# Half of one input loaded by sixteen transfers of eight partitions instead of one of 128

## The chip, the cores and the metric

One core of a Trainium2 chip. The metric is the device time of one execution in microseconds (us). A run counts as fast when it lies within 1.5% of the fastest of its kernel. Ratios are the mean time of one kernel's fast runs over the mean of the other's fast runs of the same rounds, so they are not quite the ratio of the medians quoted beside them.

## The reference, cut to what matters

```python
def _attn_ref(q, k, v):                      # each (8, 8, 576, 64) float32
    phi = lambda x: np.where(x > 0, x, np.exp(x) - 1.0) + 1.0
    q_p, k_p = phi(q), phi(k)
    kv = np.einsum('bhsd,bhse->bhde', k_p, v);  z = np.sum(k_p, axis=2)
    num = np.einsum('bhsd,bhde->bhse', q_p, kv)
    den = np.einsum('bhsd,bhd->bhs', q_p, z)[..., None] + 1e-06
    return num / den
# then: rfft over the sequence, 64 modes times complex 512 x 512 weights
# (moe_w_r, moe_w_i: 134 MB in float32), irfft, residual, u + relu(u @ w_ch)
```

The kernel reads 164 MB from memory, 134 MB of it the two weight arrays.

## The kernel before

GpSimd issues nearly all loads; they convert float32 to a 16-bit type on the way. Batch 0's q is the exception: SyncE loads it as float32 in two halves (c = 0 and 1), and then the identity and the DFT table.

```python
    def load(b):
        for nm, src in (("q", q), ("k", k), ("v", v)):
            ...
            if (nm, b) == ("q", 0):
                for c in range(2):
                    t = sA.tile([128, 2, NJ * Dh], F32, tag="x16", bufs=2, name=f"q32_{c}")
                    pin(nc.sync.dma_start(out=t, in_=rows_in[:, :, c * NJ * Dh : (c + 1) * NJ * Dh]))
                    raw[nm, b, c] = t
                pin(nc.sync.dma_start(out=id16, in_=id16_dr.ap()))
                pin(nc.sync.dma_start(out=fwd_sb, in_=fwd_dr.ap()))
                continue
            t = sA.tile(shape, F16, tag=f"{nm}16", bufs=2, name=f"{nm}16_{b}")   # two buffers
            pin(nc.gpsimd.dma_start(out=t, in_=rows_in))
    ...
    def exps(b):                 # ScalarE: exp of q, then of k
        for nm in ("q", "k"): ...
    def features(b):             # VectorE: max, min of q, then of k, then the copy of v
        for nm in ("q", "k"): ...

    load(0); load(1)
    exps(0); features(0); exps(1)
    for b in range(B):
        load(b + 2)              # its k waits until batch b's k buffer is free
        ...                      # [cut]
```

`pin` keeps the order of the program on each engine. The k load of batch 2 ("k2" below) reuses the buffer of batch 0's k. So it waits until VectorE has finished batch 0's `ke`, and VectorE does q first. Everything that GpSimd loads afterwards waits behind k2.

Of the kernel before, what the change touches and what calls it, by code (L numbers as in the profile page):

```python
# [16 lines left out]
NJ = 9  # L17
# [26 lines left out]
def kernel(  # L44
# [10 lines left out]
    nc = tc.nc  # L55

    B, H, S, Dh = q.shape
# [50 lines left out]
    pin = tc.keep_in_program_order  # L108
# [69 lines left out]
    def load(b):  # L178
        for nm, src in (("q", q), ("k", k), ("v", v)):
            rows_in = src[b].rearrange("h s d -> (h s) d").rearrange(  # L180
                "(hp r j) d -> r hp (j d)", r=128, j=2 * NJ if nm == "q" else NJ
            )
            if (nm, b) == ("q", 0):
                for c in range(2):
                    t = sA.tile([128, 2, NJ * Dh], F32, tag="x16", bufs=2, name=f"q32_{c}")
                    pin(nc.sync.dma_start(out=t, in_=rows_in[:, :, c * NJ * Dh : (c + 1) * NJ * Dh]))
                    raw[nm, b, c] = t
                pin(nc.sync.dma_start(out=id16, in_=id16_dr.ap()))
                pin(nc.sync.dma_start(out=fwd_sb, in_=fwd_dr.ap()))
                continue  # L190
            shape = [128, 2, 2 * NJ * Dh] if nm == "q" else [128, NHP, NJ * Dh]
            t = sA.tile(shape, F16, tag=f"{nm}16", bufs=2, name=f"{nm}16_{b}")
            pin(nc.gpsimd.dma_start(out=t, in_=rows_in))
            raw[nm, b] = t
# [157 lines left out]
    def transform(b, dc):  # L352
# [17 lines left out]
        if dc == NDC - 1:  # L370
# [3 lines left out]
            pin(nc.scalar.mul(out=xv[:, :, 0, :], in_=xf[:, :, 1, :], mul=-1.0))  # L374

    load(0)
    load(1)
    exps(0)
    for _ in features(0):
        pass  # L380
    exps(1)
    for b in range(B):
        if b + 2 < B:
            load(b + 2)
            if b % 2 == 1:
                w_next()
        turn_q(b, 0)
        turn_q(b, 1)
        sum_kv(b)
        if b + 1 < B:  # L390
            for _ in features(b + 1):
                pass
        if b + 2 < B:
            exps(b + 2)
        for jj in range(NJJ + 1):
            form_x(b, jj)
            if b == 0 and jj == 0:
                make_place()
            if b > 1 and jj == 1:
                place_x(b - 2)  # L400
            if b > 0 and jj in (2, 3):
                transform(b - 1, jj - 2)
        if b > 0:
            transform(b - 1, 2)
            transform(b - 1, 3)
# [153 lines left out]
    def x_of(t: int):  # L559
        if t < B * NJJ:  # L560
            return x_main[t // NJJ][:, t % NJJ, :]
        i = t - B * NJJ
        return x_tail[i // 2][:, i % 2, :]
# [364 lines left out]
    for h, eng in enumerate((nc.sync, nc.gpsimd)):  # L928
        eng.dma_start(
            out=YZ_all[64 * h : 64 * h + 64 : NF // NL].rearrange("r b z d -> r b (z d)"),  # L930
            in_=last.rearrange("p z d -> p (z d)"),
# [10 lines left out]
    def add_one(n: int, i: int):  # L942
# [8 lines left out]
            out=x_of(0), in0=accs[0][:, 0], scalar=0.0, in1=x_of(0), op0=ALU.max, op1=ALU.add  # L951
# [51 lines left out]
```

## Time and profile before

| | us |
|---|---|
| median (runs) | 425.01 (423.59 to 425.35) |
| second exp of batch 0's q starts | 6.19 |
| GpSimd issues k2 | 14.61 |
| last engine ends GpSimd's sixth load | 23.38 |

From the page of the kernel before: the busy share of the 16 DMA engines in 40 slices (9 is 90% or more), the GB/s written in each slice, SyncE's queue with its packets, and the chain of waits by engine.

```profile
DMA  9999999999999999999999999999999999995697
GB/s 215 209 209 215 207 221 201 224 209 221 218 217 221 208 215 220 218 211 217 218 217 212 221 215 217 214 219 217 215 215 216 218 212 218 218 209 113 235 400 309
q1 hardware_dynamic: 4256, 11.22, 7.2%
DMA 69%; PE 16%; DVE 4%; ACT 4%; issue 3%; POOL 2%; DVEq 0%; POOLq 0%; ACTq 0%
```

The DMA engines are the bound. Mostly they write 16-bit data and read float32, so where some 210 GB/s are written, twice as much is read. Only about the last four of 40 slices look different.

From the timeline of the kernel before, the instructions that the change touches (start, duration, engine and line, output and input, and what the engine had waited for):

```profile
0.74 0.95 SPq L186 DMA_DIRECT2D q<-in_q_dram  x2
...
6.19 1.16 ACT L213 ACTIVATE qe<-q 128x1152 f16<-128x1152 f32 x1 [0.36 <-DMA q<-in_q_dram]
...
14.61 0.77 POOL L193 DMA_DIRECT2D k<-in_k_dram  x1 [8.80 <-DVE ke L226]
...
20.28 0.98 POOL L193 DMA_DIRECT2D q<-in_q_dram  x1 [4.14 <-DVE qe L226]
```

One more reading is needed. A load is split over the DMA engines, each of which writes a completion packet of four bytes when its share is done. The trace's packet records show these, but they don't name the engine. As long as the engines are less than one load apart (2.8 us), sorting by time gives each load's first and last engine. Where they come further apart, the completions of two loads mix. There the sixth load is told by its interval: it is a q load of 16 rows of 2304 bytes per engine and comes 2.79 us after the fifth on the same engine, while a k or v load of 32 rows of 1152 bytes takes 2.84 us.

### The profile page before, as it was taken

Reading aid. Unit: us, or ns where it says so; the run is one execution under the profiler, and the core shown is the slowest. Engines: PE = TensorE matmul, PEld = TensorE weight load, DVE = VectorE, ACT = ScalarE, POOL = GpSimd, SP = SyncE. Lnnn points to the kernel's source line nnn. Section 1 sums busy time; section 2 is a strip of 40 time slices with the busy share of each in tenths; the row PEclk is TensorE's granted clock in tenths of the full one; section 3 lists DMA queues with packets and bytes.
Section 4 is the critical chain, followed back from the end, with each engine's and each line's share of the span. In section 5 each row is a group of like instructions: output and inputs, shape, how many; then the busy total and the mean of one; then the engine's idle time right before and its main releaser. Section 6 shows DMA issues by size and latency. Waiting matters only on the chain.

```text
span 423.3 us, 7890 instructions
## 1 busy us (share of the span) xinstructions
PE 268.8 (63%) x3378; PEld 146.1 (35%) x3378; DVE 215.2 (51%) x447; ACT 161.4 (38%) x253; POOL 57.0 (13%) x99
## 2 busy tenths in 40 slices
PE   1358376778417645444344778869687785997992
PEld 0247355566202322222122323324243332463320
DVE  4599489994203453354444444445353424431793
ACT  4687588844202102000000244435253432330781
POOL 4222124210000100000000001100000000030000
PEclk9999889999755555555555598878898969899997
DMA  9999999999999999999999999999999999995697
GB/s 215 209 209 215 207 221 201 224 209 221 218 217 221 208 215 220 218 211 217 218 217 212 221 215 217 214 219 217 215 215 216 218 212 218 218 209 113 235 400 309
DMA packets 20802, 93.19 MB, mean 220 GB/s; under 512 B 2080, under 2 KB 11168, under 8 KB 16480
## 3 DMA queue, kind: packets, MB, share of 16 engines
q0 software_dynamic: 16512, 81.47, 93.8%
q1 hardware_dynamic: 4256, 11.22, 7.2%
q8 instruction: 26, 0.43, 0.4%
q14 instruction: 8, 0.07, 0.0%
HBM read 163.93 MB, written 9.44 MB: 410 GB/s over the span
## 4 chain that ended last, share of the span: by engine, by line
DMA 69%; PE 16%; DVE 4%; ACT 4%; issue 3%; POOL 2%; DVEq 0%; POOLq 0%; ACTq 0%
DMA w<-in_moe_w_i_dram 54%; DMA pick_sb<-row_pick 8%; PE P L442 7%; DMA k<-in_k_dram 7%; PE acc L735 3%; PE acc L774 2%; POOL w L119 2%; ACT ke L213 2%; ACT qT L249 1%; DVE ys L452 1%; DVE x L299 1%; PE yt L460 1%; ACT qe L213 1%; PE ya L653 0%; PE eps L676 0%
## 5 line engine op out<-in xcount | busy, mean ns | idle before, releaser
L442 PE MATMUL P<-w,xt_c 64*32 64x512 bf16 (+2 forms) x1000 | 51.7, 544 | 66.4 <-DMA w<-in_moe_w_i_dram 64.9
L452 DVE CAST ys<-P 128x512 f16<-128x512 f32 x32 | 22.1, 692 | 118.0 <-PE P L442 118.0
L454 ACT CAST ys<-P 128x512 f16<-128x512 f32 x31 | 18.2, 586 | 150.2 <-PE P L442 150.2
L119 POOL DMA_DIRECT2D w<-in_moe_w_r_dram x31 | 16.5, 534 | 245.1 <-PE P L442 105.9
L442 PEld LDWEIGHTS <-xt_c 64*32 64x32 bf16 (+2 forms) x1000 | 16.8, 128 | 84.7 <-DMA w<-in_moe_w_i_dram 51.1
L676 PE MATMUL eps<-wch,xTw 128*128 128x512 f16 x144 | 43.7, 434 | 0.0
L165 PEld LDWEIGHTS <-qT 64*128 64x128 f16 (+1 forms) x640 | 22.7, 123 | 52.9 <-issue 28.7
L657 DVE TENSOR_TENSOR x_main<-ya,x_main 128x512 f32<-128x512 f32 x32 | 22.0, 689 | 19.1 <-PE ya L653 18.9
L165 PE MATMUL num<-kv,qT 64*128 64x65 f16 (+1 forms) x320 | 13.4, 208 | 28.1 <-ACT kv L272 14.6
L659 ACT CAST x16w<-x_main 128x512 f16<-128x512 f32 x32 | 19.8, 618 | 25.0 <-DVE x_main L657 24.0
L684 ACT CAST E<-eps 128x512 f16<-128x512 f32 (+1 forms) x40 | 21.2, 541 | 11.2 <-PE eps L676 11.0
L165 PE MATMUL nw<-kv,qT 64*128 64x65 f16 (+1 forms) x320 | 19.0, 240 | 9.5 <-DVE x_tail L620 4.3
L460 PE MATMUL yt<-pick_sb,ys 128*128 128x16 f16 x252 | 11.7, 174 | 18.7 <-DMA pick_sb<-row_pick 12.1
L299 DVE TENSOR_TENSOR x<-num,rd 128x512 f16<-128x512 f32 x32 | 22.1, 692 | 1.1
L213 ACT ACTIVATE qe<-q 128x1152 f16<-128x1152 f16 (+1 forms) x16 | 17.8, 1156 | 10.5 <-DMA q<-in_q_dram 10.4
L249 ACT COPY qT<-qTp 128x1152 f16<-128x1152 f16 x16 | 19.7, 1298 | 0.2 <-PE qTp L242 0.2
L460 PEld LDWEIGHTS <-ys 128*128 128x128 f16 x252 | 9.7, 102 | 28.8 <-DVE ys L452 15.3
L242 PE MATMUL qTp<-id,qe 128*128 128x128 f16 x144 | 13.1, 264 | 10.0 <-DVE qe L226 9.5
L213 ACT ACTIVATE ke<-k 128x1152 f16<-128x1152 f16 x16 | 17.7, 1153 | 4.7 <-DMA k<-in_k_dram 4.7
L784 ACT ACTIVATE acc<-acc 128x512 f32<-128x512 f32 x34 | 18.1, 581 | 2.4 <-PE acc L735 1.5
L676 PEld LDWEIGHTS <-xTw 128*128 128x128 f16 x144 | 14.1, 110 | 12.6 <-issue 6.2
L119 POOL DMA_DIRECT2D w<-in_moe_w_i_dram x31 | 17.2, 555 | 4.8 <-DMA q<-in_q_dram 2.5
(114 smaller groups left out, 450.8 us busy)
## 6 DMA issues: line engine op xcount, KB each, us to landing
w<-in_moe_w_r_dram POOLq DMA_DIRECT2D x31, 1024.0 KB, 12.4
w<-in_moe_w_i_dram POOLq DMA_DIRECT2D x31, 1024.0 KB, 16.8
out_dram<-x_main SPq DMA_DIRECT2D x11, 512.0 KB, 4.8
k<-in_k_dram POOLq DMA_DIRECT2D x8, 576.0 KB, 12.7
v<-in_v_dram POOLq DMA_DIRECT2D x8, 576.0 KB, 14.8
q<-in_q_dram POOLq DMA_DIRECT2D x7, 576.0 KB, 12.7
out_dram<-x_main SPq DMA_DIRECT2D x6, 256.0 KB, 4.8
q<-in_q_dram SPq DMA_DIRECT2D x2, 576.0 KB, 4.4
```

Of the source, the lines that this page charges most:

```text
L119: nc.gpsimd.dma_start(out=w_in[p][half::2], in_=two.rearrange("g (r dc) e -> (g r) dc e", dc=NDW))
L165: mm = nc.tensor.matmul(num[hpo][orow, c0 : c0 + 65], qT[rows, hpp, h2, cols], kv_sb[rows, hpp, h2, :])
L213: pin(nc.scalar.activation(out=ev[:, c], in_=heads(nm, b, c), func=AF.Exp))
L249: nc.scalar.copy(out=qT[:, :, c * NJ : (c + 1) * NJ], in_=qT_ps.rearrange("p j x -> p x j"))
L299: nc.vector.tensor_tensor(out=dst.rearrange("p (o c d) -> p o c d", o=2, c=4), in0=nv[:, :, :, 0:64], in1=rden.unsqueeze(3).broadcast_to([ ...
L442: nc.tensor.matmul(P[c : c + n, :], xt_cols(dc, kk, n), w[rows, dc, :], start=(dc < NDC), stop=(dc >= n_dc - NDC), tile_position=(rows.sta ...
L452: pin(nc.vector.tensor_copy(out=st, in_=P))
L460: nc.tensor.matmul(yt_ps[:, ec, kk % 8, :], st[:, ec * 128 : ec * 128 + 128], pick_sb)
L657: pin(nc.vector.tensor_tensor(out=x, in0=acc, in1=x, op=ALU.add))
L659: pin(nc.scalar.copy(out=x16w[t], in_=x))
L676: nc.tensor.matmul(e_ps, xT[:, c, :], wch16[:, c, :], start=(c == 0), stop=(c == NDC - 1))
L684: pin(nc.scalar.copy(out=dst, in_=e_ps[:, cols]))
```

## The change

It cuts the second half of batch 0's q into sixteen transfers of eight partitions each, 36 KB instead of 576 KB. It doesn't say what for; smaller pieces might land earlier or leave more room for GpSimd's loads.

```diff
-                    pin(nc.sync.dma_start(out=t, in_=rows_in[:, :, c * NJ * Dh : (c + 1) * NJ * Dh]))
+                    rows_c = rows_in[:, :, c * NJ * Dh : (c + 1) * NJ * Dh]
+                    step = 128 if c == 0 else 8
+                    for r in range(0, 128, step):
+                        pin(nc.sync.dma_start(out=t[r : r + step], in_=rows_c[r : r + step]))
```

The order of instructions on the other engines is unchanged. Only waits are added: SyncE reuses eight completion semaphores, so its ninth issue waits for the first to land, and so on; the second exp waits for eight semaphores.

## The prediction

> **What bounds the kernel.** The DMA engines. The page's slices show DMA at nine tenths or more in nearly every slice until the last few, and the chain of waits is 69% DMA (54% the w_i loads). In the trace's packet records the completion packets of GpSimd's loads come with a constant pitch: 2.84 us for each k, v or q load of 576 KB, 4.85 us for each w half of 1024 KB, from 8.9 us to about 375 us. GpSimd's queue never runs dry in between (w loads take 12.4 and 16.8 us to land, so two to three are always waiting). The records of one load show all 16 engines within 0.4 us at first and 3.4 us apart at the end: an engine that falls behind stays behind, and a load lands with its last engine.
>
> **What the change does.** One transfer of 576 KB (issued at 1.2 us, landing about 6.2 us) becomes sixteen of 36 KB; c = 0 is unchanged. The built program has eight completion semaphores for SyncE's loads, so the eighth small transfer waits for c = 0, the ninth for the first small one, and so on; the identity and the DFT table follow the sixteenth. ScalarE's exp and VectorE's max of the second half now wait for all eight semaphores.
>
> Cost on SyncE: 432 to 455 ns per issue in the timeline, so about 16 x 0.45 = 7.2 us instead of 0.45. The last issue should be near 8 us, the landing at 9.5 to 11.5 us (c = 0 took 3.9 us). The second exp, which started at 6.19 us, starts 3.5 to 5 us later; VectorE is in order, so both minima and ke slip, and GpSimd's k2 load, issued at 14.6 us after ke, goes out at about 17 to 19 us. But the queue already holds loads until 23 us (the sixth ends there), so it does not run dry: this delay is absorbed. ScalarE's next work waited for q1's landing (3.46 us idle before 15.28), which also swallows it; form_x of batch 0 starts within 0.5 us of its 23.7.
>
> **What remains.** The Trainium skill, page "DMA: Bandwidth & Descriptors", section on why a DMA increments its semaphore by 16, says that the slowest dimension decides the engine count: eight partitions use eight engines, the lowest-numbered. The trace of before has no such transfer. Then those eight move 32 rows of 2304 B each instead of 16 (93 ns each: +1.5 us), and the others none. Much of the second half now moves after GpSimd's packets begin at 5 us: about ten small transfers x 2 rows x 93 ns = 1.9 us on eight engines, against about 0.5 us on all of them before. So eight engines get about 1.2 to 1.5 us behind, the others 0.5 us ahead, and that stays to the end. It reaches the total if the slowest engines at the end (about eight lie 3.0 to 3.4 us behind) include one of those eight, probably; if all are among the others, nothing, or half a microsecond gained.
>
> **Predicted: 426.2 us**, 8 in 10 between 424.9 and 427.5. Chances: faster by over 2% 0.005, within 2% 0.98, slower by over 2% 0.015.
>
> **Signs.** SyncE's queue: 4256 packets become 4368 (eight engines: 112 more completion packets) or 4496 (sixteen engines). Second exp at 10 to 11.5 us; k2's issue at 17 to 19; w's pitch still 4.85 us; spread of the first k load's completion packets up from 0.4 to 1.5 to 2 us; the last w landing about 1 us later.
>
> **What would make it wrong.** Small transfers landing so slowly beside GpSimd's that k2's issue passes 20 us: the queue empties and each further microsecond counts. Or the spread of engines closing again.

## More of the kernel before

GpSimd has issued its first six loads by 5.8 us. They keep the DMA engines busy until 23 us, so k2 at 14.61 us joins a queue with almost 9 us of work in it. The stretches of time around 23 us confirm that (columns: the stretch, its length, busy time of PE, PEld, DVE, ACT and POOL with instruction counts, granted clock, DMA share, GB/s written):

```profile
10.00:17.00 7.00, 3.89 (x51) 3.18 (x49) 3.54 (x5) 3.54 (x4) 1.52 (x2) 1.00 1.17 209
...
22.00:24.00 2.00, 0.88 (x24) 0.87 (x24) 1.47 (x4) 1.48 (x4) 0.90 (x2) 1.00 1.13 205
24.00:26.00 2.00, 0.55 (x14) 0.25 (x8) 1.97 (x10) 1.99 (x2) 1.34 (x2) 1.00 1.21 208
26.00:28.00 2.00, 1.47 (x19) 1.34 (x19) 1.90 (x7) 1.34 (x2) 0.00 (x0) 1.00 1.21 207
```

## The result, and the profile after

429.04 us median (428.12 to 430.24) against 425.01: ratio 1.0103, 95% interval 1.0065 to 1.014. That is within 2%, but clearly slower, and above the predicted range.

From the page after, the same lines:

```profile
DMA  9999999999999999999999999999999999995797
GB/s 195 204 150 225 197 212 210 216 224 217 213 219 218 213 211 216 220 213 219 219 215 211 220 214 219 219 209 216 220 214 221 217 213 213 219 211 109 243 403 288
q1 hardware_dynamic: 4368, 11.23, 7.5%
DMA 65%; PE 18%; DVE 6%; issue 3%; ACT 3%; POOL 2%; SPq 0%; DVEq 0%; POOLq 0%; ACTq 0%
```

The third slice of GB/s (21.4 to 32.1 us) has fallen to 150; the busy digits hide it. SyncE's queue has 112 packets more, which is 16 x 8 - 16: every small transfer has eight completion packets. That agrees with the Trainium skill, page "DMA: Bandwidth & Descriptors", section "Why a DMA increments its semaphore by 16 and not by 1", by which eight partitions use eight engines.

From the timeline after:

```profile
0.74 10.05 SPq L189 DMA_DIRECT2D q<-in_q_dram  x17
...
17.40 1.16 ACT L216 ACTIVATE qe<-q 128x1152 f16<-128x1152 f32 x1 [11.02 <-DMA id<-ident]
...
24.56 1.11 POOL L196 DMA_DIRECT2D k<-in_k_dram  x1 [18.74 <-DVE ke L229]
```

The second exp starts at 17.40 us, not 6.19 (the releaser named there is not its own: the exp waits for the small q transfers, the last of which wrote its completions at 16.39). So VectorE's `ke` is late, and k2 is issued at 24.56 instead of 14.61, after GpSimd's queue has been used up on eight of the engines (they end the sixth load by 22.62). The stretches after:

```profile
10.00:17.00 7.00, 0.00 (x0) 0.00 (x0) 0.00 (x0) 0.00 (x0) 0.00 (x0) 1.00 1.28 194
...
22.00:24.00 2.00, 1.09 (x9) 0.92 (x10) 1.97 (x4) 2.00 (x3) 0.00 (x0) 1.00 0.72 126
24.00:26.00 2.00, 1.25 (x24) 1.25 (x25) 1.97 (x4) 2.00 (x3) 1.44 (x2) 1.00 0.56 107
26.00:28.00 2.00, 1.18 (x23) 0.91 (x20) 1.97 (x4) 1.95 (x5) 1.07 (x2) 1.00 0.78 94
```

From 22 to 28 us the engines move about half of what they moved before. The packet records date the loss and show that it stays (completion packets, first engine to last engine, us):

```
                         before             after             last engine
GpSimd's 1st load     8.88 to   9.28     6.90 to   9.06          -0.2
6th load             22.98 to  23.38    22.23 to  27.24          +3.9
7th load (k2)        25.83 to  26.23    30.03 to  31.92          +5.7
11th load            37.14 to  38.39    41.35 to  43.24          +4.9
last w load                to 389.42          to 393.66          +4.2
```

There are two suspects by 28 us. The queue had nothing to do because k2 was late. But the eight engines that carried the small transfers were also late by themselves: they ended the sixth load at 26.4 to 27.2 us, the other eight at 22.2 to 22.6.

### The profile page after: what moved, and what is told of

Its sections match the earlier page's. It is cut to its first block, busy times and chain, and to the rows that moved or that the text cites. A ratio compares the mean times of both kernels' runs of the same rounds, so it can differ in the third digit from the quotient of the medians.

```text
span 428.5 us, 7919 instructions
## 1 busy us (share of the span) xinstructions
PE 272.7 (64%) x3378; PEld 149.9 (35%) x3378; DVE 215.1 (50%) x447; ACT 161.4 (38%) x253; POOL 56.1 (13%) x99
## 3 DMA queue, kind: packets, MB, share of 16 engines
q1 hardware_dynamic: 4368, 11.23, 7.5%
## 4 chain that ended last, share of the span: by engine, by line
DMA 65%; PE 18%; DVE 6%; issue 3%; ACT 3%; POOL 2%; SPq 0%; DVEq 0%; POOLq 0%; ACTq 0%
DMA w<-in_moe_w_i_dram 50%; PE P L445 8%; DMA pick_sb<-row_pick 7%; DMA k<-in_k_dram 3%; PE acc L738 3%; DMA q<-in_q_dram 3%; PE acc L777 2%; POOL w L119 1%; DMA fwd_sb<-dft_fwd 1%; ACT ke L216 1%; DVE qe L229 1%; PE z L701 1%; DVE ys L455 1%; DVE q L223 1%; DVE x L302 1%
## 5 line engine op out<-in xcount | busy, mean ns | idle before, releaser
L445 PE MATMUL P<-w,xt_c 64*32 64x512 bf16 (+2 forms) x1000 | 53.0, 556 | 67.6 <-DMA w<-in_moe_w_i_dram 66.2
L679 PE MATMUL eps<-wch,xTw 128*128 128x512 f16 x144 | 41.5, 417 | 0.0
L245 PE MATMUL qTp<-id,qe 128*128 128x128 f16 x144 | 16.0, 300 | 21.2 <-DVE qe L229 20.7
L165 PE MATMUL num<-kv,qT 64*128 64x65 f16 (+1 forms) x320 | 13.7, 209 | 20.8 <-ACT xt_c L353 11.2
L245 PEld LDWEIGHTS <-qe 128*128 128x128 f16 x144 | 13.8, 140 | 22.3 <-DVE qe L229 21.1
L463 PE MATMUL yt<-pick_sb,ys 128*128 128x16 f16 x252 | 11.7, 174 | 15.3 <-DMA pick_sb<-row_pick 8.7
L679 PEld LDWEIGHTS <-xTw 128*128 128x128 f16 x144 | 13.7, 107 | 11.7 <-issue 4.4
```

The costliest lines, as they stand in the source:

```text
L165: mm = nc.tensor.matmul(num[hpo][orow, c0 : c0 + 65], qT[rows, hpp, h2, cols], kv_sb[rows, hpp, h2, :])
L245: nc.tensor.transpose(qT_ps[:, j], phi["q", b][:, c, j].rearrange("p o d -> p (o d)"), id16,)
L445: nc.tensor.matmul(P[c : c + n, :], xt_cols(dc, kk, n), w[rows, dc, :], start=(dc < NDC), stop=(dc >= n_dc - NDC), tile_position=(rows.sta ...
L463: nc.tensor.matmul(yt_ps[:, ec, kk % 8, :], st[:, ec * 128 : ec * 128 + 128], pick_sb)
L679: nc.tensor.matmul(e_ps, xT[:, c, :], wch16[:, c, :], start=(c == 0), stop=(c == NDC - 1))
```

## The experiments

All gave correct results. The last three columns are from one profiled run each, the last of them from its packet records. The kernel before was run beside each group of four.

| kernel | median, us | ratio to before, 95% interval | second exp | k2 issued | 6th load, first to last engine |
|---|---|---|---|---|---|
| before | 424.76, 424.94, 423.78 | | 6.19 | 14.61 | 22.98 to 23.38 |
| the change | 429.04 | 1.0103 [1.0065, 1.0140] | 17.40 | 24.56 | 22.23 to 27.24 |
| e1 sixteen, 16 engines | 427.45 | 1.0073 [1.0043, 1.0102] | 15.12 | 22.28 | 23.16 to 24.38 |
| e2 eight, 16 engines | 425.27 | 1.0035 [0.9994, 1.0075] | 11.70 | 18.85 | 23.18 to 25.49 |
| e3 two, 7 and 9 engines | 426.67 | 1.0077 [1.0033, 1.0120] | 11.43 | 18.59 | 22.60 to 26.62 |
| e4 the change, k first | 428.74 | 1.0110 [1.0082, 1.0137] | 17.71 | 15.30 | 22.60 to 27.58 |
| e5 before, k first | 424.76 | 1.0002 [0.9975, 1.0028] | | 14.74 | 23.13 to 23.50 |
| e6 e1, k first | 425.33 | 1.0029 [0.9985, 1.0074] | | 14.99 | 23.26 to 25.33 |
| e7 unread copy, sixteen | 430.08 | 1.0107 [1.0062, 1.0152] | 6.37 | 16.52 | 23.97 to 28.79 |
| e8 unread copy, one | 426.73 | 1.0047 [1.0027, 1.0068] | 6.31 | 15.94 | 24.73 to 25.15 |
| e9 the change, spread | 429.56 | 1.0127 [1.0104, 1.0149] | 17.34 | 24.50 | 21.71 to 25.20 |
| e10 e9, k first | 426.78 | 1.0062 [1.0037, 1.0087] | 17.12 | 13.03 | 21.67 to 25.12 |
| e11 half of it, k first | 424.24 | 1.0015 [0.9975, 1.0054] | | 14.78 | 22.41 to 25.06 |
| e12 unread copy, spread | 426.45 | 1.0052 [1.0027, 1.0077] | 6.43 | 16.33 | 23.13 to 26.94 |

In the profiled runs of e2 and e6 one engine was 1.8 us behind the rest (in e6: fifteen engines by 23.54, one at 25.33), and in e11 one was 0.7 us behind. Each of these was the slowest of its kernel's four runs. What held that engine up is open; the medians are little touched, but the ratios, which use means, are raised by it. The profiled runs of the change, e7, e9 and e12 were also the slowest of their four, that of e3 the fastest (425.48 us), so a trace and a median need not agree to a microsecond.

### First group: why is the half late, and is its lateness the cost?

**e1, sixteen transfers over sixteen engines each.**

```diff
-                    for r in range(0, 128, step):   # step 8 for c = 1
-                        pin(nc.sync.dma_start(out=t[r : r + step], in_=rows_c[r : r + step]))
+                    for r in range(0, 128 * c, 16):
+                        for o in range(2):
+                            pin(nc.sync.dma_start(out=t[r : r + 16, o], in_=rows_c[r : r + 16, o]))
```

> Second half of q by sixteen transfers still, each of 36 KB, same rows of 2304 B, same waits on the eight semaphores, but cut so that sixteen partitions (and so sixteen engines) share each: one row per engine. Theory E (the cost is eight engines carrying all rows beside GpSimd's stream): the second exp starts at 9.5 to 12 us instead of 17.4, k2's load is issued before 20 us, the total is 424.5 to 426. Theory C (the cost is the number of transfers, with their completion writes and semaphore waits): second exp near 17 us, k2 near 24 us, total 428 to 430. SyncE's queue: 4496 packets in both.

The packets are 4496, as expected. The second exp started at 15.12 us and the total was 427.45. Both theories missed, theory E by more. From its timeline:

```profile
15.12 1.16 ACT L218 ACTIVATE qe<-q 128x1152 f16<-128x1152 f32 x1 [9.08 <-DMA q<-in_q_dram]
...
22.28 1.11 POOL L198 DMA_DIRECT2D k<-in_k_dram  x1 [16.46 <-DVE ke L231]
```

So 8.9 of the 11.2 us of lateness come with the number of transfers even when no engine has an extra row to carry. Most of that is SyncE's own time: the sixteen issues run from 1.25 to 10.5 us, 1.6 us of it waits for earlier ones to land. The last goes out at 10.1 us and lands at 14.3, 4.2 us later, although it is so small; one large transfer, issued at 1.2, landed at 5.7. The packet records show that the small ones move slowly: between 9 and 10 us, with about five of them issued and not landed, SyncE's queue got 33 rows through and GpSimd's 143, while one large transfer in the same place (e8) got 84 against 84. A small transfer does not hold its place beside a busy queue. The engines themselves lost little: the sixth load ended at 24.38, all but one by 23.7.

**e2, eight transfers of sixteen partitions.**

```diff
-                    step = 128 if c == 0 else 8
+                    step = 128 if c == 0 else 16
```

> Eight transfers of sixteen partitions: sixteen engines each, two rows per engine per transfer. Theory E: second exp at 7.5 to 9.5 us, total as before, 424.5 to 425.5. Theory C: half of the delay remains, second exp 10 to 12 us, k2 at about 19 us, total 425 to 426.5. SyncE's queue: 4368 packets in both.

Second exp at 11.70 and k2 at 18.85, as theory C had it. The total is not clear of before.

**e3, two transfers on seven and nine engines.**

```diff
-                    for r in range(0, 128, step):
-                        pin(nc.sync.dma_start(out=t[r : r + step], in_=rows_c[r : r + step]))
+                    for r in (slice(0, 128),) if c == 0 else (slice(0, 119), slice(119, 128)):
+                        pin(nc.sync.dma_start(out=t[r], in_=rows_c[r]))
```

> Two transfers only, of 119 and 9 partitions. If the engine count is the largest divisor up to sixteen, the first runs on seven engines with 34 rows each, the second on nine with two each. Theory E: as bad as the change or worse: second exp at 15 to 20 us, k2 at 22 to 27 us, total 428 to 432. Theory C: two completions and no semaphore wait on SyncE, so second exp at 8 to 11 us, total 425 to 426.5. SyncE's queue: 4256 packets if the engine counts are seven and nine.

The packets are 4256. Nine engines end the sixth load at 22.60 to 22.93 us and seven at 26.07 to 26.62, so the division into seven and nine holds. The second exp is at 11.43 us, near theory C's span and far from theory E's. Yet the time is longer than before: the last of the seven engines ended the sixth load 3.2 us late. 20 rows more (x 93 ns = 1.9 us) explain part of that; between 8 and 10 us q's rows also took longer, 0.16 us in the median instead of 0.106 (e1). k2 at 18.59 left no gap. This is a cost of uneven engines without a late k2.

**e4, the change with k first.**

```diff
     def exps(b):
-        for nm in ("q", "k"):
+        for nm in ("q", "k") if b else ("k", "q"):
     # features(b) the same, with the copy of v right after k
```

> The changed loads as they are, but ScalarE and VectorE do batch 0's k (and v) before its q, so GpSimd's k2 and v2 loads no longer wait behind the late half of q. Theory A (the time is lost because k2 is issued too late and GpSimd's queue runs empty): k2 at 15 to 17 us, no gap in the queue at 23 to 28 us, total 425 to 426.7. Theory B (the time is lost on the eight engines themselves, which finish the first six loads at 27.2 us instead of 23.4): k2 as early, but the sixth load still ends near 27 us and the total is 428 to 430.

Theory A, that the late k2 is the whole cause, falls. From e4's timeline and stretches:

```profile
15.30 0.77 POOL L196 DMA_DIRECT2D k<-in_k_dram  x1 [9.48 <-DVE ke L236]
```

```profile
10.00:17.00 7.00, 0.00 (x0) 0.00 (x0) 2.97 (x5) 3.27 (x3) 0.77 (x1) 1.00 1.28 190
...
22.00:24.00 2.00, 1.88 (x25) 1.55 (x25) 1.97 (x4) 1.70 (x2) 0.00 (x0) 1.00 1.17 206
24.00:26.00 2.00, 1.47 (x28) 1.20 (x23) 1.75 (x3) 2.00 (x3) 0.70 (x1) 1.00 1.17 210
26.00:28.00 2.00, 0.65 (x24) 0.66 (x24) 1.57 (x4) 1.46 (x3) 0.70 (x1) 1.00 1.17 207
```

k2 goes out at 15.30 us, the gap is gone, and the total is as long as ever, 428.74. Without the gap the sixth load still ends at 27.58. And from 10 to 17 us, where nothing was starved, the engines moved 190 GB/s against e1's 230 in the next fence. Both carry the same bytes.

```profile
10.00:17.00 7.00, 0.00 (x0) 0.00 (x0) 0.69 (x2) 1.88 (x2) 0.00 (x0) 1.00 1.17 230
...
24.00:26.00 2.00, 1.20 (x28) 0.93 (x25) 1.97 (x4) 1.95 (x4) 0.83 (x2) 1.00 0.99 126
```

### Second group: controls, and the burden by itself

**e5, the kernel before with k first.** The edit is e4's.

> The control for the k-first order: the kernel before with batch 0's k and v ahead of its q on ScalarE and VectorE, loads untouched. If the order itself costs nothing: total within 0.5 us of the kernel before, last w landing within 0.5 us. If the order itself is what kept the k-first run at 428.7: total 426.5 to 429.

The order costs nothing (1.0002).

**e6, sixteen transfers over sixteen engines with k first.** The edits are e1's and e4's.

> The sixteen transfers over all sixteen engines together with the k-first order. There the late k2 (22.3 us) left a gap and all engines were even. If that gap is what the wide form cost (2.7 us): k2 at 15 to 16 us, no gap, total within 0.7 us of the kernel before. If the sixteen transfers cost time by themselves: total 426.5 to 428 as without the order.

The median fell from 427.45 to 425.33, within the expected 0.7 us of before; the intervals of e1 and e6 still overlap. By the medians the late k2 was most or all of the cost in the even form.

**e7, sixteen more transfers that nobody reads.** The same half of q is loaded once more into memory that is written for real only at 44 us.

```diff
                 pin(nc.sync.dma_start(out=fwd_sb, in_=fwd_dr.ap()))
+                copy = xt_c[:, 0 : 4 * NJ * Dh].bitcast(F32).rearrange("p (o f) -> p o f", o=2)
+                for r in range(0, 128, 8):
+                    pin(nc.sync.dma_start(out=copy[r : r + 8], in_=rows_in[r : r + 8, :, NJ * Dh :]))
```

> The kernel before, plus sixteen more transfers of eight partitions (the same half of q again) into memory that nothing reads, issued after the DFT table: the burden on eight engines by itself, 32 rows x 93 ns = 3.0 us, with no one waiting for it. Second exp stays at 6.2 us and k2 at 14 to 16 us. If the slowest engine decides the end: last w landing and total 2.5 to 3.5 us later. If the sixteen engines share the burden: 1.5 us later. If nothing but the late half of q cost time: no change.

From its timeline, the exp and k2:

```profile
6.37 1.16 ACT L216 ACTIVATE qe<-q 128x1152 f16<-128x1152 f32 x1 [0.32 <-DMA q<-in_q_dram]
...
16.52 1.10 POOL L196 DMA_DIRECT2D k<-in_k_dram  x1 [10.70 <-DVE ke L229]
```

Nothing that is awaited is late enough to leave a gap, and the kernel is still 5 us slower by the medians (2.6 to 6.5 us by the interval of the ratio), against an estimate of 3.0 us for the rows. In the profiled run the eight burdened engines ended the sixth load at 28.39 to 28.79, 5.4 us late, which is more than their rows account for. The other eight ended it at 23.97 to 24.27, only 0.9 us late: they were not kept back to the pace of the slow ones. But they were hindered a little: between 17 and 19 us, when they alone still had rows of 1152 bytes to write, these took about 0.13 us in the median and up to 0.23 instead of 0.107.

**e8, the same copy by one transfer.** As e7, with one transfer of 128 partitions.

> The same bytes again by one transfer of 128 partitions: 16 rows x 93 ns = 1.5 us on each of sixteen engines, nobody waits. Total and last w landing 1.2 to 1.8 us later if the DMA engines are the bound throughout; the difference to the narrow copy is the price of using eight engines.

Ratio 1.0047, which is 2.0 us, just above the expected 1.2 to 1.8, and the sixteen engines stayed together. Added DMA work shows in the total at about its own size.

### Third group: neighbours

In the change, between 10 and 13 us, q's rows took 0.22 us in the median (most 0.16 to 0.25) and completion packets up to 0.75 us. In e1 they took 0.106 and 0.022. So the small transfers on eight engines had something in their way.

**e9, every sixteenth partition instead of eight neighbours.**

```diff
-                    step = 128 if c == 0 else 8
-                    for r in range(0, 128, step):
-                        pin(nc.sync.dma_start(out=t[r : r + step], in_=rows_c[r : r + step]))
+                    step = 1 if c == 0 else 16
+                    for r in range(step):
+                        pin(nc.sync.dma_start(out=t[r::step], in_=rows_c[r::step]))
```

> The changed kernel, but each of the sixteen transfers takes every sixteenth partition instead of eight neighbours: same count, same eight engines, same rows. Theory P (neighbouring partitions make the eight engines collide where they write, which shows in completion packets of up to 0.75 us and rows of 0.2 us in the changed kernel against 0.02 and 0.106 in the sixteen-engine form): rows near 0.11 us, longest completion under 0.1 us, second exp at 12 to 15.5 us, total 426 to 427.5. Theory B (only the number of rows per engine counts): nothing changes, second exp 16.5 to 18 us, total 428.3 to 430.

The rows took 0.106 us and the completions 0.022, as theory P said. The second exp and the total stayed where they were, as theory B said. The stretches tell why:

```profile
10.00:17.00 7.00, 0.00 (x0) 0.00 (x0) 0.00 (x0) 0.00 (x0) 0.00 (x0) 1.00 1.16 228
...
22.00:24.00 2.00, 1.03 (x9) 0.87 (x9) 1.97 (x4) 2.00 (x3) 0.00 (x0) 1.00 0.65 123
24.00:26.00 2.00, 1.31 (x26) 1.31 (x27) 1.97 (x3) 2.00 (x3) 1.50 (x2) 1.00 0.28 53
```

The engines now move 228 GB/s from 10 to 17 us and are done with the sixth load by 25.2, and then they wait for k2 (24.50 us). At 24 to 26 us they move 53 GB/s, half of what the changed kernel moved there. What was saved on the engines was spent waiting. The exp came no earlier in part because the edit has a side effect: each spread transfer takes SyncE 0.59 us to issue, most of the change's take 0.27 to 0.30, so the last goes out at 11.7 us instead of 10.5.

**e10, spread and k first.** The edits are e9's and e4's.

> The same spread transfers with batch 0's k ahead of its q, so that no gap in GpSimd's queue mixes in; to compare with the k-first run at 428.7. Theory P: last completion of the sixth load at 25 to 26 us instead of 27.3, total 425.8 to 427.2. Theory B: 27 us and 428 to 429.5.

```profile
13.03 1.11 POOL L196 DMA_DIRECT2D k<-in_k_dram  x1 [7.21 <-DVE ke L236]
```

```profile
10.00:17.00 7.00, 0.00 (x0) 0.00 (x0) 3.52 (x5) 1.29 (x2) 1.86 (x2) 1.00 1.16 227
...
24.00:26.00 2.00, 1.33 (x36) 1.08 (x32) 1.97 (x4) 1.85 (x4) 0.70 (x1) 1.00 1.18 206
```

Only with both removed does the time fall, to 426.78 (1.0062). The sixth load's last engine is at 25.12, 1.74 us after before's; 16 more rows of 93 ns on eight engines would be 1.49 us. The interval of the total is 1.6 to 3.7 us over before.

**e11, half the dose, k first.** The edit cuts partitions 0 to 63 into eight neighbours each and loads 64 to 127 at once, with e4's order.

> Half the dose, k first: partitions 0 to 63 by eight transfers of eight neighbours, 64 to 127 by one transfer on sixteen engines. Eight engines then carry 24 rows instead of 16 (32 in the full form). If the cost grows with the rows or the number of narrow transfers: about half of the 4 us, total 426 to 427.3, sixth load's last completion 24.8 to 25.8 us. If any narrow transfers cost the whole: 428 or more.

The last engine of the sixth load is at 25.06 us as expected, but that is the one straggler; the others ended by 24.3. The total, 424.24, is better than expected and not distinct from before (interval 0.9975 to 1.0054). By the medians the cost falls faster than by half; the intervals allow a half as well.

**e12, the unread copy, spread.** As e7, with every sixteenth partition.

> The unread copy by sixteen transfers on eight engines, each of every sixteenth partition; to compare with the copy by neighbours (430.1, about 5 us over before). Theory P: 427 to 428.5, that is the 3.0 us of 32 more rows or less. Theory B: 429 to 431.

426.45 us, at 1.0052 less than half of e7's excess, a little under what theory P expected. The pairs e4/e10 and e7/e12 point the same way. Within each pair the intervals overlap a little (e4 starts at 1.0082, e10 ends at 1.0087; e7 starts at 1.0062, e12 ends at 1.0077), but the packet durations, the 190 against 227 GB/s and the last engine of the sixth load (27.58 against 25.12, 28.79 against 26.94) are plain.

### What it comes to

| | neighbours | spread |
|---|---|---|
| q first (k2 at 24.5 us) | 429.04 | 429.56 |
| k first (k2 at 13 to 15 us) | 428.74 | 426.78 |

Two delays run side by side up to 27 us. One is the late second half, which holds back k2 through two engines that work in order, until GpSimd's queue is empty. The other is the hindrance of eight engines by transfers of neighbouring partitions. Taking either one away leaves the other, which ends at nearly the same time: in the change k2's first completion, 30.03 us, less the 2.84 us of one load, puts the start of k2's data at an estimated 27.2 us, and the hindered engines end the sixth load at 27.24. That is why e4 and e9, each of which plainly removed its suspect, gained nothing. Under both lies the uneven split, 1.7 us (e10).

No version beat the kernel before; k first alone equals it.

One thing about the hindrance stays open, what neighbours collide on: the Trainium skill, page "SBUF — State Buffer", section "Door 1: The DMA port swizzle", says that four neighbouring partitions share a port, so eight neighbours reach two ports and every sixteenth partition four. But e1's sixteen neighbours on sixteen engines put as many engines on each port as the change does, and its rows took 0.106 us, so that map alone does not explain it, and the reading side changed as well.

## Why the prediction was right or wrong

- **The bound: right.** The pitch of the w halves stayed 4.85 us, and what was lost by 28 us was still missing at the end (+4.2 us at the last w load). e8 confirmed that DMA work counts in full.
- **Eight engines: right.** 4368 packets.
- **"The last issue should be near 8 us, the landing at 9.5 to 11.5 us": this step failed.** The last issue was at 10.5 us, the last completion at 16.4, the exp at 17.40. The estimate counted issue time and one landing, and gave small transfers the same chance beside GpSimd's queue as a large one. In the run SyncE waited 4.0 us for small transfers to land before it could issue the next, and the last took 5.9 us from issue to landing. e1 shows most of the lateness with the number of transfers.
- **"It does not run dry: this delay is absorbed": failed in consequence.** k2 went out at 24.56 us instead of 17 to 19, and e1, e6 and e9 show what the gap then costs. The prediction did name this as the way in which it would be wrong, with 20 us as the limit; it was given too little weight.
- **"Eight engines get about 1.2 to 1.5 us behind": right in size where it stands alone** (e10: 1.74 us, a little above). In the change it was not the term that mattered, and it lacked the hindrance by neighbours (e4: 27.58 us against e10's 25.12).
- **"The others 0.5 us ahead, and that stays to the end": right up to the gap, then wrong.** They ended the sixth load at 22.23 to 22.62 us, 0.8 us ahead of the kernel before, and then had nothing to do until k2 came.
- The spread of the first k load's completions was 2.16 us, near the predicted 1.5 to 2.

## What to carry to other kernels

A transfer that is first in a chain on in-order engines should be few and wide: sixteen transfers of 36 KB landed 11 us later than one of 576 KB, because SyncE needs time to issue each, and because beside a busy queue each small one loses its place. The Trainium skill says in "DMA: Bandwidth & Descriptors", section "Rules for kernel authors", to coalesce small transfers, since under 64 KB one pays mostly overhead. As to the landing these runs agree; the engines' own time hardly grew where the sixteen were spread evenly (e6: ratio 1.0029, not clear of before). When the DMA queue is the bound, ask by when the next issue must come so that it does not empty, and when a cause is taken away and nothing improves, look for a second one that ends at the same time before dropping the first.

## What the Trainium skill lacked or had wrong

- "DMA: Bandwidth & Descriptors", section "Queues, rings and completion order", says that an engine takes turns between queues at packet granularity. It has no figure for small transfers: one large transfer got 84 rows to GpSimd's 84 in a microsecond (e8), sixteen small ones 33 to 143 (e1). Landing times were about 5.7 us for one, 10.4 for eight (without the straggler), 14.3 for sixteen wide, and 16.4 for sixteen on eight engines.
- No page read for this has a figure for the hindrance of transfers of eight neighbouring partitions on eight engines beside a busy queue; the port map named above comes nearest. Here: rows of 0.22 us in the median instead of 0.106, completions up to 0.75 us instead of 0.022.
- The rule for the engine count in "Why a DMA increments its semaphore by 16 and not by 1" held for 8, 16, 119 and 9 partitions (4368, 4496 and 4256 packets).
